# Attention with a sink and a window, then a leaky-ReLU MLP: preparing a chunk one stage earlier, in six transposes at a time, and a ramp written out by hand

## The chip, the core and the metric

The kernel runs on one NeuronCore of one Trainium2 chip. Times are device microseconds of one execution. A NeuronCore has TensorE (PE, matrix products into PSUM; PEld is its loading of weights), VectorE (DVE), ScalarE (ACT), GpSimd (POOL) and SyncE (SP, which here only issues DMAs). Each engine works through its own instructions in program order and waits for others by semaphores. PSUM has eight banks of 128 partitions x 2 KB, SBUF is the working memory.

## The reference

```python
scores = 1/sqrt(64) * q @ k.T              # q, k, v: (4, 8, 768, 64)
causal = rel >= 0                           # rel = query position - key position
stream_keep = causal & (key < 4 | rel < 64) # 4 sink keys, a window of 64
mask = causal where is_retrieval[head] else stream_keep   # is_retrieval = [1,0,1,0,0,0,1,0]
a = softmax(where(mask, scores, -1e9))
x = (a @ v), heads side by side             # (3072, 512)
h = x @ w_in                                # 512 -> 2048
out = max(0.01 * h, h) @ w_out              # 2048 -> 512
```

The list of flags says which heads are retrieval heads: 0, 2 and 6 see all earlier keys, the other five ("stream" heads) see four sink keys and a window of 64.

## The kernel before

**Chunks.** The 3072 rows are cut into eight chunks of 384 tokens, two per sequence; chunk n belongs to sequence n // 2 and is its first half (even n) or second half (odd n). Each chunk goes through four kinds of work:

- *Load and cast.* SP loads k, q and v of a chunk as float32 into four rotating buffers `f` (L66 to L82). POOL casts them to bfloat16 (`cast_chunk`, L199 to L210); v goes straight into `va`. A copy of v moved by 64 tokens, `vb`, is made by two DMAs on ACT's queue (`v_shift`, L192).
- *Preparation* (`prep_slots`, L212). For each of four pairs of heads, PE transposes k (three products with the identity, L221) into the bank `pt`; DVE copies one head's half to `kt` (L237), ACT the other (L235); then PE transposes q, and DVE copies it to `qt` (L229). `pt` is one bank with two halves; chunks 0 and 1 also use the bank `py` (`pt_tile`).
- *Attention* (`attention_slots`). A unit is one tile of scores: products into `psS` (L312 for retrieval, L347 for stream heads), the exponential on ACT (L317, L352), a mask on DVE (L321, L356), and two units later the product with v into the bank `po` (L261). An even chunk has 12 units, an odd one 21, one of which is the sink unit: DVE picks the sink keys (`ksink`, L280), PE scores them (L284). When a pair is complete, DVE divides by the sums (L373, L375), and two slots later PE transposes the result and ACT copies it to `xt` (`x_t`, L381, L382).
- *MLP.* `in_slots`: 16 steps of four products (L435) with leaky ReLU on ACT into `g` (L437). `out_slots`: 16 steps of two to four products (L449) that fill three 128-row tiles in the bank `py`; DVE copies each tile (L460), SP stores it.

PSUM's eight banks: two each for `ph` (MLP input), `psS` and `po`, one each for `py` and `pt`.

**The order.** It is written out by hand (`manual_schedule`); nothing reorders instructions afterwards, and the framework only adds the semaphores. `merge(ms, as_)` spreads one list of steps evenly over another. The stages, with chunk 0 alone first: attention of 0; input of 0 merged with preparation and attention of 1; input of 1; output of 0 merged with preparation and attention of 2; then for n = 2 to 7 the steps of input n and output n-1 in turn, merged with preparation and attention of n+1; last, output of 7. So a chunk is prepared at the start of the stage in which its attention runs. POOL also issues the weight loads, which cast while they move: half of `w_in` after the first v cast, the other half after chunk 1's q cast, then `w_out`. In the last tile of output 7 DVE copies one half and ACT the other, and two queues store them.

Of the kernel before, what the change touches and what calls it, by code (L numbers as in the profile page):

```python
# [21 lines left out]
def kernel(  # L22
# [23 lines left out]
    NCH = B * (S // CH)  # L46

# [4 lines left out]


    WIDE = 2
    qw = q.rearrange("b h (c p g) d -> b c p h (g d)", g=3, p=128)
    kw = k.rearrange("b h (c p g) d -> b c p h (g d)", g=3, p=128)
    qr = q.rearrange("b h (c g p) d -> b c p h g d", g=3, p=128)
    kr = k.rearrange("b h (c g p) d -> b c p h g d", g=3, p=128)
    vr = v.rearrange("b h (c g p) d -> b c p h g d", g=3, p=128)
# [6 lines left out]
    def load(n, nm, half=None):  # L66
        b, c = divmod(n, 2)
        if half != 1:
            stage[nm, n] = rot.tile([128, 3 * H * D], FP32, name="f", tag="f", bufs=4)
        t = stage[nm, n]  # L70
        if nm == "v" or n >= WIDE:
            tv = t.rearrange("p (g h d) -> p g h d", g=3, h=H)
            for g in range(3):
                nc.sync.dma_start(out=tv[:, g], in_={"q": qr, "k": kr, "v": vr}[nm][b, c, :, :, g])
            return
        hs = slice(0, H) if half is None else slice(4 * half, 4 * half + 4)
        src = (qw if nm == "q" else kw)[b, c]
        nc.sync.dma_start(out=t.rearrange("p (h x) -> p h x", h=H)[:, hs], in_=src[:, hs])

    def load_chunk(n):  # L80
        for nm in "kqv":
            load(n, nm)  # L82
# [18 lines left out]
    ident = one.tile([128, 128], BF16, name="ident")  # L101
    make_identity(nc, ident)
    m_win0 = one.tile([128, 6, 64], BF16, name="m_win0")

    kt = [one.tile([128, 4, 2, S], BF16, name=f"kt{i}") for i in range(2)]
    va = [one.tile([128, 6, H, D + 1], BF16, name=f"va{i}") for i in range(2)]
    vb = [one.tile([128, 5, H, D + 1], BF16, name=f"vb{i}") for i in range(2)]
    vs = [one.tile([128, H, D + 1], BF16, name=f"vs{i}") for i in range(2)]
    ksink = [one.tile([128, 4, 128], BF16, name=f"ksink{i}") for i in range(2)]
    ats = [one.tile([128, 3, 4, 64], BF16, name=f"ats{i}") for i in range(4)]  # L110
    w_in_bf = one.tile([128, KG, DF], BF16, name="w_in_bf")
    w_out_bf = one.tile([128, NG, DM], BF16, name="w_out_bf")

    def late_constants():
        nc.vector.tensor_copy(m_win0[:, 2:], m_win[:, 2:])
        nc.vector.tensor_copy(m_win0[:, 0, :], m_caus[:, 0:64])
        nc.vector.tensor_copy(m_win0[:, 1, :], m_win[:, 1, :])
        nc.vector.memset(m_win0[0:NS, 1, :], 1.0)
        nc.vector.tensor_copy(
            e_sink[:, 0 : 4 * H].rearrange("p (h r) -> p h r", r=NS),  # L120
            ident[:, 0:NS].rearrange("p (o r) -> p o r", o=1).to_broadcast([128, H, NS]),
        )

    def zeros(i):
        eng = nc.vector if i == 0 else nc.gpsimd
        eng.memset(kt[i][64:128, :, 0, :], 0.0)
        eng.memset(kt[i][0:64, :, 1, :], 0.0)
        nc.gpsimd.memset(ksink[i][:], 0.0)
        nc.gpsimd.memset(va[i][:, :, :, D], 1.0)
        nc.gpsimd.memset(vs[i][:, 0, :], 0.0)  # L130

    zeros(0)
    m_caus = one.tile([128, 128], BF16, name="m_caus")
    nc.gpsimd.memset(m_caus[:], 1.0)
    nc.gpsimd.affine_select(
        out=m_caus[:], in_=m_caus[:], compare_op=ALU.is_ge, fill=0.0,
        base=0, channel_multiplier=-1, pattern=[[1, 128]],
    )
    m_win = one.tile([128, 6, 64], BF16, name="m_win")
    nc.gpsimd.memset(m_win[:], 1.0)  # L140
    nc.gpsimd.affine_select(
        out=m_win[:], in_=m_win[:], compare_op=ALU.is_gt, fill=0.0,
        base=0, channel_multiplier=1, pattern=[[0, 6], [-1, 64]],
    )
    nc.gpsimd.affine_select(
        out=m_win[:], in_=m_win[:], compare_op=ALU.is_ge, fill=0.0,
        base=64, channel_multiplier=-1, pattern=[[0, 6], [1, 64]],
    )
    for a in ats:
        nc.gpsimd.memset(a[:, :, 1:3, :], 0.0)  # L150

    e_sink = one.tile([128, 128], BF16, name="e_sink")
    nc.gpsimd.memset(e_sink[:], 0.0)
    m_sink = one.tile([128, H, D + 1], BF16, name="m_sink")
    nc.gpsimd.memset(m_sink[:], 1.0)
    nc.gpsimd.affine_select(
        out=m_sink[:], in_=m_sink[:], compare_op=ALU.is_ge, fill=0.0,
        base=0, channel_multiplier=1, pattern=[[-NS, H], [0, D + 1]],
    )
    nc.gpsimd.affine_select(  # L160
        out=m_sink[:], in_=m_sink[:], compare_op=ALU.is_ge, fill=0.0,
        base=NS - 1, channel_multiplier=-1, pattern=[[NS, H], [0, D + 1]],
    )
    for h in range(H):
        if IS_RETR[h]:
            nc.gpsimd.memset(m_sink[:, h, :], 0.0)

    pt_n = [0]  # L170
    pt_bank = ps.tile([128, 2, 4, 128], BF16, name="pt", tag="pt", bufs=1)

    def pt_tile(n):

        pt_n[0] += 1
        if n <= 1 and pt_n[0] % 3 == 2:
            return ps.tile([128, 8, 128], BF16, name="py", tag="py", bufs=1)
        return pt_bank[:, pt_n[0] % 2]
# [4 lines left out]
    def qk_src(nm, n):  # L183
        if n >= WIDE:
            return stage[nm, n].rearrange("p (g h d) -> p g h d", h=H, g=3)
        return stage[nm, n].rearrange("p (h g d) -> p g h d", h=H, g=3)

    def cast_tile(nm, n):
        cast[nm, n] = rot.tile([128, 3, H, D], BF16, name=f"{nm}b", tag=f"{nm}b", bufs=2)
        return cast[nm, n]  # L190

# [7 lines left out]
    def cast_chunk(n, between=None):  # L199
        b, c = divmod(n, 2)  # L200
        i = b % 2
        for nm in "kq":
            tb, src = cast_tile(nm, n), qk_src(nm, n)
            for g in range(3):
                nc.gpsimd.tensor_copy(tb[:, g], src[:, g])  # L205
        if between:
            between()
        src = stage["v", n].rearrange("p (g h d) -> p g h d", g=3, h=H)
        for g in range(3):
            nc.gpsimd.tensor_copy(va[i][:, 3 * c + g, :, 0:D], src[:, g])  # L210

    def prep_slots(n):  # L212
        b, c = divmod(n, 2)
        i = b % 2
        qts[n] = rot.tile([128, 4, CH], BF16, name="qt", tag="qt", bufs=2)

        def one_pair(nm, p):
            pt = pt_tile(n)
            tb = cast[nm, n]
            for g in range(3):  # L220
                nc.tensor.transpose(pt[:, g, :], tb[:, g, 2 * p : 2 * p + 2, :], ident[:])  # L221
            pv = pt[:, 0:3, :]
            tok = lambda ap: ap.rearrange("p (g t) -> p g t", g=3)
            if n < WIDE:

                pv = pv.rearrange("p g t -> p t g")
                tok = lambda ap: ap.rearrange("p (t g) -> p t g", g=3)
            if nm == "q":
                nc.vector.tensor_copy(tok(qts[n][:, p, :]), pv)  # L229
                return  # L230
            for hh in range(2):
                r = slice(64 * hh, 64 * hh + 64)
                dst = tok(kt[i][r, p, hh, CH * c : CH * c + CH])
                if hh == 1:
                    nc.scalar.activation(out=dst, in_=pv[r], func=ACTF.Copy)  # L235
                else:
                    nc.vector.tensor_copy(dst, pv[r])  # L237

        return [lambda nm=nm, p=p: one_pair(nm, p) for p in range(4) for nm in "kq"]
# [5 lines left out]
    def attention_slots(n):  # L245
        b, c = divmod(n, 2)
        i = b % 2
        qt = lambda: qts[n]
        xts[n] = rot.tile([128, 4, CH], BF16, name="xt", tag="xt", bufs=2)
        q0 = CH * c  # L250
        po = {}
        at_sink = {}

        def av(p, hh, qi, lhsT, rhs, first, last):
            if p not in po:
                po[p] = ps.tile([128, 3, 2, D + 1], FP32, name="po", tag="po", bufs=2)
                first = True
            else:
                first = False
            o = po[p][:, qi, :, :] if hh is None else po[p][:, qi, hh, :]  # L260
            nc.tensor.matmul(o, lhsT=lhsT, rhs=rhs, start=first, stop=last, skip_group_check=True)  # L261

        sc = [0]

        def score():
            sc[0] += 1
            tag = "ph" if n == 0 and sc[0] % 2 else "psS"
            return ps.tile([128, 512], FP32, name=tag, tag=tag, bufs=2)

        units = []  # L270

        sink_lo = 128 if c == 0 else 0

# [296 lines left out]
```

## Time and profile before

| | us |
|---|---|
| median of 3 runs (lowest to highest) | 288.99 (288.77 to 289.32) |
| the profiled execution, its own time | 289.96 |
| span of its trace | 288.3 |
| PE busy in it | 249.1 (86%) |
| ACT, DVE, POOL busy | 152.4, 105.2, 59.1 |

The span runs from the first to the last instruction of one execution; the time around it is larger. Busy time of PE includes the modelled ends of its products, so that a busy PE isn't PE at its peak. The page also gives the span in 40 slices of 7.2 us, with the TensorE clock that was granted in tenths of full speed. Stretches are named by microseconds from the span's start. In this execution the stages end at about 31 (attention of chunk 0), 58 (input 0 with chunk 1), 69.5 (input 1), 96.5 (output 0 with chunk 2), 129, 158, 191, 220 and 252 (the loop, n = 2 to 6), 274 (n = 7) and 284.5 (output 7). In a line of the waits, "X <- Y: a, b, c" says that X waited a us in total for Y, b times, at longest c us.

### The profile page before, as it was taken

To read this page: it belongs to the slowest core of one execution; us is meant where nothing else is said; L and a number is where in the kernel's file an instruction comes from. 1 tells how busy PE (TensorE), PEld (TensorE's weight loads), DVE (VectorE), ACT (ScalarE), POOL (GpSimd) and SP (SyncE) were. 2 spreads that over 40 slices of the span, in tenths; PEclk is the share of its full clock that TensorE was granted. 3 is DMA by queue.
4 is the path that set the end of the run, shared out by engine and by line. 5 is a ranking of instruction groups with operands and counts; after the bars stand their busy time and mean duration, and the time that the engine had idled before them with its cause. 6 is when DMAs were issued, how large, how long until landed. Compare 5 with 4: busy or idle time off the path is not lost.

```text
span 288.3 us, 5327 instructions
## 1 busy us (share of the span) xinstructions
PE 249.1 (86%) x2111; PEld 149.2 (52%) x2140; DVE 105.2 (36%) x298; ACT 152.4 (53%) x329; POOL 59.1 (21%) x102
## 2 busy tenths in 40 slices
PE   1275699898778899999899899999898899999994
PEld 0155366554345456665466456655565466655541
DVE  6556334500246322533553333333453234311021
ACT  3345278776135457764566467745564567643300
POOL 8518930650000043002400151004300000000000
PEclk9997579999699999999999999999999999999999
DMA  8999999991000596009910990149413001010012
GB/s 188 285 261 226 208 207 210 218 191 33 6 36 36 111 228 121 36 16 218 210 38 2 211 224 23 39 95 228 118 39 82 13 36 39 0 39 36 36 73 73
DMA packets 75720, 32.36 MB, mean 112 GB/s; under 512 B 63280, under 2 KB 71728, under 8 KB 75696
## 3 DMA queue, kind: packets, MB, share of 16 engines
q1 hardware_dynamic: 70048, 25.04, 40.9%
q0 software_dynamic: 4224, 4.19, 8.6%
q10 hardware_dynamic: 1424, 2.79, 4.5%
q8 instruction: 16, 0.26, 0.4%
q14 instruction: 8, 0.07, 0.1%
HBM read 27.26 MB, written 6.29 MB: 116 GB/s over the span
## 4 chain that ended last, share of the span: by engine, by line
PE 75%; DVE 10%; ACT 8%; issue 3%; DMA 1%; ACTq 1%; DVEq 0%
PE py L449 25%; PE ph L435 25%; PE po L261 6%; PE pt L221 6%; PE psS L312 4%; ACT kt L235 4%; DVE kt L237 3%; PE pt L381 2%; PE psS L449 2%; PE psS L347 2%; ACT ats L352 2%; DVE xs L375 2%; PE psS L284 1%; DVE o L460 1%; DMA f<-in_k_dram 1%
## 5 line engine op out<-in xcount | busy, mean ns | idle before, releaser
L435 PE MATMUL ph<-xt,w_in_bf 128*128 128x384 bf16 x512 | 104.6, 331 | 0.1
L449 PE MATMUL py<-w_out_bf,g 128*128 128x512 bf16 x324 | 91.5, 386 | 2.1 <-DVE o L460 0.4
L437 ACT ACTIVATE g<-ph 128x384 bf16<-128x384 f32 x128 | 62.9, 492 | 48.6 <-PE ph L435 46.9
L435 PEld LDWEIGHTS <-w_in_bf 128*128 128x128 bf16 x512 | 46.1, 99 | 27.4 <-issue 2.6
L449 PEld LDWEIGHTS <-g 128*128 128x128 bf16 x384 | 33.9, 99 | 25.2 <-issue 2.8
L317 ACT ACTIVATE at<-psS 128x384 bf16<-128x384 f32 x81 | 39.2, 492 | 12.4 <-PE psS L312 12.2
L205 POOL CAST kb<-f 128x512 bf16<-128x512 f32 x21 | 12.8, 617 | 109.0 <-DMA f<-in_k_dram 109.0
L321 DVE TENSOR_TENSOR at<-at,m_caus 128x128 bf16<-128x128 bf16 x72 | 15.9, 248 | 40.9 <-ACT at L317 40.8
L235 ACT ACTIVATE kt<-pt 64x384 bf16<-64x384 bf16 x30 | 14.6, 486 | 30.1 <-DVE kt L237 29.8
L460 DVE COPY o<-py 128x512 f32<-128x512 f32 x21 | 14.5, 690 | 36.0 <-PE py L449 34.9
L312 PE MATMUL psS<-qt,kt 128*128 128x384 bf16 (+2 forms) x105 | 26.8, 295 | 0.1
L261 PE MATMUL po<-va,at 128*128 128x65 bf16 x252 | 22.1, 197 | 1.0 <-DVE at L321 1.0
L237 DVE COPY kt<-pt 64x384 bf16<-64x384 bf16 x30 | 11.7, 389 | 26.8 <-PE pt L221 26.8
L356 DVE TENSOR_TENSOR ats<-ats,m_win 128x384 bf16<-128x384 bf16 x40 | 15.1, 377 | 15.2 <-ACT ats L352 14.7
L382 ACT ACTIVATE xt<-pt 128x384 bf16<-128x384 bf16 x30 | 14.7, 489 | 10.8 <-PE pt L381 10.5
L221 PE MATMUL pt<-ident,qb 128*128 128x128 bf16 x84 | 10.3, 237 | 11.6 <-ACT kt L235 10.6
L229 DVE COPY qt<-pt 128x384 bf16<-128x384 bf16 x28 | 10.8, 384 | 25.7 <-PE pt L221 25.7
L261 PEld LDWEIGHTS <-at 128*128 128x128 bf16 x252 | 16.6, 100 | 6.8 <-DVE at L321 1.6
L352 ACT ACTIVATE ats<-psS 128x384 bf16<-128x384 f32 x37 | 17.9, 491 | 2.8 <-PE psS L347 2.8
L221 PEld LDWEIGHTS <-qb 128*128 128x128 bf16 x96 | 8.9, 111 | 20.1 <-issue 16.0
L205 POOL CAST qb<-f 128x512 bf16<-128x512 f32 x21 | 13.1, 629 | 27.1 <-DMA f<-in_q_dram 20.3
L221 PEld LDWEIGHTS <-kb 128*128 128x128 bf16 x96 | 9.0, 110 | 18.2 <-DVE kb L496 8.2
(75 smaller groups left out, 231.6 us busy)
## 6 DMA issues: line engine op xcount, KB each, us to landing
f<-in_v_dram SPq DMA_DIRECT2D x24, 256.0 KB, 5.4
out_dram<-o SPq DMA_DIRECT2D x23, 256.0 KB, 2.0
f<-in_k_dram SPq DMA_DIRECT2D x18, 256.0 KB, 5.3
f<-in_q_dram SPq DMA_DIRECT2D x18, 256.0 KB, 5.2
w_in_bf<-in_moe_w_in_dram POOLq DMA_DIRECT2D x4, 512.0 KB, 9.1
w_out_bf<-in_moe_w_out_dram POOLq DMA_DIRECT2D x4, 512.0 KB, 15.6
vb<-va ACTq DMA_DIRECT2D x8, 195.0 KB, 3.5
vb<-va ACTq DMA_DIRECT2D x8, 130.0 KB, 2.9
```

Of the source, the lines that this page charges most:

```text
L205: nc.gpsimd.tensor_copy(tb[:, g], src[:, g])
L221: nc.tensor.transpose(pt[:, g, :], tb[:, g, 2 * p : 2 * p + 2, :], ident[:])
L235: nc.scalar.activation(out=dst, in_=pv[r], func=ACTF.Copy)
L237: nc.vector.tensor_copy(dst, pv[r])
L261: nc.tensor.matmul(o, lhsT=lhsT, rhs=rhs, start=first, stop=last, skip_group_check=True)
L312: nc.tensor.matmul(s[:, off : off + w], lhsT=kt[i][:, p, hh, 128 * kj : 128 * kj + 128], rhs=qt()[:, p, lo:CH], start=(j == 0), stop=(j == ...
L317: nc.scalar.activation(out=a[:, 0:off], in_=s[:, 0:off], func=ACTF.Exp, scale=SM)
L352: nc.scalar.activation(out=av_, in_=s[:, 0:CH].rearrange("p (j e f) -> p j e f", j=3, e=2), func=ACTF.Exp, scale=SM)
L435: nc.tensor.matmul(ph[:, 0:CH], lhsT=w_in_bf[:, g, 128 * t : 128 * t + 128], rhs=xts[n][:, g, :], start=(g == 0), stop=(g == KG - 1))
L437: nc.scalar.activation(out=gs[n][:, t, :], in_=ph[:, 0:CH], func=ACTF.Prelu, alpha=0.01)
L449: nc.tensor.matmul(py[n][:], lhsT=gs[n][:, ng, 128 * tt : 128 * tt + 128], rhs=w_out_bf[:, ng, :], start=(ng == 0), stop=(ng == NG - 1))
L460: nc.vector.tensor_copy(o[:], py[n][:])
```

## The change

It concerns four places.

- *Preparation.* `prep_pair` transposes k and q of a pair together, six products into one bank, and then copies three pieces out; by default all three copies are DVE's. A chunk from 4 on is prepared one stage ahead, in four steps: one before the first attention slot of the chunk before it, the others behind the x transposes of a pair (`slots(extra)`). Chunk 2 is prepared ahead of its own attention, in the merged list; chunk 3 in four steps with nothing between, after chunk 2's attention. Casts and loads move one chunk ahead too.
- *Ramp.* The order of chunk 0's attention and chunk 1's preparation is written out, with transposes in `pt`, `py` and `ph`, and copies shared between DVE and ACT by a string ("vva": two on DVE, one on ACT). The second half of chunk 0's casts comes after the first scores. Weights are loaded after chunk 1's q cast; chunk 2 is loaded from POOL's queue.
- *Order of the MLP.* Eight input steps of chunk 0 are merged with chunk 1's attention; the rest and input 1 follow, then the whole output of chunk 0 in `py` and `ph`. Nine output steps of chunk 1 are merged with chunk 2, seven go into the loop.
- *Shift and end.* Chunk 0's `vb` is made by products with two shift matrices (`v_shift_pe`), four of them per tile, copied by ACT. The last tile of output 7 is computed in two halves of 256 columns in two banks.

```diff
+    def v_shift_pe():
+        for t in range(2):
+            p = bank("po", [128, 512], FP32)
+            w = D + 1
+            for o, hs in ((0, slice(1, 8, 2)), (4 * w, slice(4, 5))):
+                n = len(range(*hs.indices(8))) * w
+                for e in range(2):
+                    nc.tensor.matmul(p[:, o : o + n], lhsT=shift[:, e, :], rhs=va[0][:, t + e, hs, :],
+                                     start=(o == 0 and e == 0), stop=(e == 1), skip_group_check=True)
+            src = p[:, 0 : 4 * w].rearrange("p (h d) -> p h d", h=4)
+            nc.scalar.activation(out=vb[0][:, t, 1:8:2, :], in_=src, func=ACTF.Copy)
+            nc.scalar.activation(out=vb[0][:, t, 4, :], in_=p[:, 4 * w : 5 * w], func=ACTF.Copy)
+
+    def prep_pair(n, p, tag="pt", eng=("v", "v", "v")):
...
+        pt = bank(tag, [128, 2, 4, 128], BF16)
+        for e, nm in enumerate("kq"):
+            for g in range(3):
+                nc.tensor.transpose(pt[:, e, g, :], cast[nm, n][:, g, 2 * p : 2 * p + 2, :], ident[:])
...
+        for hh in range(2):
+            r = slice(64 * hh, 64 * hh + 64)
+            move(eng[hh], kt[i][r, p, hh, CH * c : CH * c + CH], pt[r, 0, 0:3, :])
+        move(eng[2], qts[n][:, p, :], pt[:, 1, 0:3, :])
...
+        def slots(self, extra=()):
...
+            if extra:
+                r.append(extra.pop(0))
+            for t in range(len(units) + LAG + 2):
...
+                r.append(slot)
+                if extra and t in [last[p] + LAG + 2 for p in range(4)]:
+                    r.append(extra.pop(0))
+            return r + extra
...
         for tt in range(3):
+            if halves and tt == 2:
+                slots.append(lambda: part(2, 0, NG, "py", 0, 256))
+                slots.append(lambda: part(2, 0, NG, "psS", 256, 512))
+                continue
...
-    for f in attention_slots(0):
-        f()
-    cast_chunk(1, between=lambda: [load_w("in", i) for i in (2, 3)])
-    v_shift(1)
-    for i in range(4):
-        load_w("out", i)
-    load_chunk(2)
-    zeros(1)
-    merge(in_slots(0), prep_slots(1) + attention_slots(1))
-    for f in in_slots(1):
-        f()
-    cast_chunk(2)
-    v_shift(2)
-    load_chunk(3)
-    merge(out_slots(0), prep_slots(2) + attention_slots(2))
+    a0 = Attention(0, ("psS", "ph"))
+    cast_half(0)
+    prep_pair(0, 0, "pt", "vva")
+    prep_pair(0, 1, "py", "aav")
+    u = [a0.units[h] for h in range(H)]
+    first = u[0] + u[2]
+    run([x[0] for x in first])
+    nc.gpsimd.tensor_copy(va[0][:, 0, :, 0:D], v_src(0)[:, 0])
+    nc.vector.tensor_copy(va[0][:, 1, :, 0:D], v_src(0)[:, 1])
+    nc.gpsimd.tensor_copy(va[0][:, 2, :, 0:D], v_src(0)[:, 2])
+    late_constants()
+    run([x[0] for x in u[1] + u[3]])
+    sink_mask()
+    cast_qk(1)
+    for i in range(4):
+        load_w("in", i)
+    cast_v(1)
+    for i in range(4):
+        load_w("out", i)
+    load_chunk(2, nc.gpsimd)
+    v_shift_pe()
+    run([x[1] for x in first])
+    cast_half(1)
+    prep_pair(0, 2, "pt", "vva")
+    prep_pair(0, 3, "py", "aav")
+    a0.sink()
+    second = u[4] + u[5] + u[6] + u[7]
+    run([second[0][0]], [x[1] for x in u[1] + u[3]], [second[1][0]])
+    xs0 = a0.finish(0)
+    run([second[2][0]])
+    xs1 = a0.finish(1)
+    run([second[3][0]])
+    a0.x_t(0, xs0, "pt")
+    run([second[0][1], second[4][0], second[1][1]])
+    a0.x_t(1, xs1, "py")
+    xs2 = a0.finish(2)
+    run([x[1] for x in second[2:]])
+    xs3 = a0.finish(3)
+    prep_pair(1, 0, "pt", "vva")
+    a0.x_t(2, xs2, "py")
+    prep_pair(1, 1, "ph", "aav")
+    a0.x_t(3, xs3, "pt")
+    prep_pair(1, 2, "py", "vva")
+    prep_pair(1, 3, "ph", "aav")
+    v_shift(1)
+    a1 = Attention(1).slots()
+    in0, in1 = in_slots(0), in_slots(1)
+    run(a1[0:8], merge(in0[0:8], a1[8:]))
+    zeros(1)
+    run(in1[0:8], in0[8:12], in1[8:12], in0[12:16], in1[12:16])
+    run(out_slots(0, ("py", "ph", "py")))
+    cast_qk(2)
+    cast_v(2)
+    v_shift(2)
+    load_chunk(3)
+    out1 = out_slots(1)
+    a2 = preps(2) + Attention(2).slots()
+    run(merge(out1[0:9], a2))
+    cast_qk(3)
+    cast_v(3)
+    v_shift(3)
+    load_chunk(4)
+    run(preps(3))
+    outs = out1[9:]

     for n in range(2, NCH):
         a = []
-        if n + 1 < NCH:
-            cast_chunk(n + 1)
-            v_shift(n + 1)
-            if n + 2 < NCH:
-                load_chunk(n + 2)
-            a = prep_slots(n + 1) + attention_slots(n + 1)
-        merge(weave(in_slots(n), out_slots(n - 1)), a)
-    for f in out_slots(NCH - 1, ("psS", "psS", "py"), True):
-        f()
+        if n + 2 < NCH:
+            cast_qk(n + 2)
+            cast_v(n + 2)
+            if n + 3 < NCH:
+                load_chunk(n + 3)
+        if n + 1 < NCH:
+            a = Attention(n + 1).slots(preps(n + 2) if n + 2 < NCH else ())
+        run(merge(merge(in_slots(n), outs), a))
+        if n + 2 < NCH:
+            v_shift(n + 2)
+        outs = out_slots(n) if n + 1 < NCH else out_slots(n, ("psS", "psS", "py"), True)
+    run(outs)
```

## The prediction

> **What bounds the kernel now.** I read the page's first two parts first, then the windows cut where the stages begin, then PE's waits, then the timeline of one preparation.
>
> ```profile
> PE 249.1 (86%) x2111; PEld 149.2 (52%) x2140; DVE 105.2 (36%) x298; ACT 152.4 (53%) x329; POOL 59.1 (21%) x102
> PE   1275699898778899999899899999898899999994
> PEclk9997579999699999999999999999999999999999
> ```
>
> PE is the bound: no other engine passes 53%. The 39 us that it isn't busy lie in the first 14 slices and at the end, and in two places its clock sinks. The stages (columns: stretch, its length, then PE, PEld, DVE, ACT, POOL busy, clock, DMA share, GB/s):
>
> ```profile
> 0.00:31.10 31.10, 13.63 (x136) 9.83 (x137) 18.15 (x46) 12.89 (x24) 19.75 (x44) 0.91 1.13 237
> ...
> 69.50:80.40 10.90, 8.07 (x39) 4.03 (x39) 2.47 (x7) 2.44 (x5) 0.00 (x0) 0.69 0.11 26
> 80.40:96.50 16.10, 13.12 (x144) 7.57 (x146) 9.01 (x32) 7.23 (x16) 0.00 (x0) 1.00 0.09 34
> ...
> 273.80:284.50 10.70, 10.51 (x48) 4.57 (x47) 2.18 (x4) 0.29 (x1) 0.00 (x0) 1.00 0.20 74
> ```
>
> Chunk 0's attention takes 31.1 us for 13.6 us of products; chunk 2's stage (69.5 to 96.5) 27.0 us. A dense output phase needs 10.5 us for 48 products, 0.219 each; 57.7 to 69.5 has 18 input steps in 11.8, 0.656 each. The preparations of the later stages, cut out alone:
>
> ```profile
> 96.50:105.10 8.60, 7.17 (x51) 4.05 (x52) 3.33 (x9) 3.91 (x8) 1.52 (x3) 1.00 1.09 206
> 129.00:138.20 9.20, 8.53 (x61) 4.88 (x60) 3.34 (x10) 4.40 (x9) 2.10 (x4) 1.00 1.14 211
> 158.00:167.00 9.00, 7.29 (x53) 4.12 (x53) 3.43 (x9) 4.18 (x9) 1.68 (x3) 1.00 1.05 200
> 190.80:200.00 9.20, 8.55 (x62) 4.89 (x61) 3.35 (x10) 4.40 (x9) 2.15 (x4) 1.00 1.15 212
> 220.00:228.90 8.90, 7.19 (x53) 4.06 (x52) 3.38 (x9) 4.22 (x9) 0.00 (x0) 1.00 0.28 74
> ```
>
> Length less PE busy: 1.43 + 0.67 + 1.71 + 0.65 + 1.71 = 6.2 us idle. The attention behind them loses 0.16 us where the chunk is odd, 1.0 and 1.3 where it is even. The wait, and one occurrence:
>
> ```profile
> PE pt L221 <- ACT kt L235: 10.8, 22, 1.2
> ...
> 160.94 0.35 DVE L237 COPY kt<-pt 64x384 bf16<-64x384 bf16 x1 [0.42 <-PE pt L221]
> 161.33 0.49 ACT L235 ACTIVATE kt<-pt 64x384 bf16<-64x384 bf16 x1 [1.13 <-DVE kt L237]
> 161.86 0.33 PE L221 MATMUL pt<-ident,qb 128*128 128x128 bf16 x3 [0.31 <-ACT kt L235]
> ```
>
> Three transposes, a copy on DVE, then one on ACT, and only then the next three: all on one bank, one after the other.
>
> **What the Trainium skill says.** "PSUM — Partial Sum Buffer", section "PSUM bank collisions raise a hardware error", has two engines on one bank kept apart by semaphores; the trace agrees: ACT starts 0.04 us after DVE ends, though their halves differ. "TensorE: Matmul & The Clock Gate", Part 1, has the clock halved after a window of some 3.4 us with little work, and back after a busy one. Agreed: four input products take 1.28 us at 35.2 us and 0.65 later, and after 69.5 to 73.2 us (PE some 37% occupied) the clock is 0.69. "DMA: Bandwidth & Descriptors", "Issuing engines are not separate DMA queues": loads on another queue share the same engines and save only issue time.
>
> **The change, part by part.** Times are from the span's start, and durations are rows above or timeline entries.
>
> *Preparation between scores (chunks 4 to 7).* Six transposes, then three copies on DVE, set behind the x transposes of a pair, a whole stage before use. Between x_t and a preparation there lies an input or output step (0.65) and a score; the x copy on ACT takes 0.49, so the bank is mostly free in time. DVE takes 4 x 0.36 more per stage and ACT 4 x 0.49 less (DVE 11 to 13 us busy of 29 to 33: room). Of 6.2 us I leave 1.2 (bounds 0 and 6.2). The even chunks' attention gets 31 steps to 20 slots, now 31 to 25 with eight preparations: 0.9 less idle. Stage n=2 is worse: only 23 steps beside 26 attention slots and four preparations; 39.6 to 57.7 shows what thin cover does (some 15.3 us of work in 18.1). For 24 us of work I charge 1.3. Sum **-4.6**.
>
> *The block of chunks 2 and 3.* Output of chunk 0 now runs dense, 10.5. Chunk 2's four pairs meet one bank: six transposes 0.50, then 0.35 + 0.35 + 0.36 on DVE, a cycle of 1.55 with overlap; three cycles, the last transposes and an output step: 5.6. Its attention took 16.1 with 11 output steps; seven are left, 2.6 us less work, of which I take 1.4 off, because the waits that they covered (ksink 1.1, xs 0.7 and 0.5 there) stay: 14.7. Then chunk 3's four pairs stand alone, followed by the first of chunk 4 on the same bank: 0.5 for the last x copy and four cycles, 6.7. Together 37.5, against 27.0 now. For that 28 output products (6.1) and five pairs (1.7) are done ahead: **+2.7** net. In the lone pairs PE does 1.7 us in 6.7, so its clock must fall: one window of 3.4 us at half speed in dense work, 1.7, and 0.5 for the first block (43% occupied, partly beside waits of its own): **+2.2** (bounds 0.5 and 5).
>
> *The ramp.* Followed from 5.5 us. Both operands of a pair now share a bank, so its copies start at 7.0 instead of 6.07 and go DVE, DVE, ACT. First scores 8.7 (now 15.1). DVE then has six masks, the V cast, six constants and two window masks before the second k cast: 14.3 (now 11.1). ACT has the four copies of the shift products (1.2 to 1.3 us for two DMAs of 2.9 to 3.5 that go) before the second q cast: done 15.5 (now 13.3). Pairs 2 and 3, DVE and ACT in turn: 19.1. ksink 19.1 to 19.8 (now 19.5 to 20.2): the early scores are paid back here. The rest of chunk 0, xs of the last pair at 28.6 (now 30.0); twelve copies of chunk 1 and two x copies on two engines, end 34.4; two DMA issues on ACT, first exponential of chunk 1 at 35.2. Now that point is 39.6, but with four input steps (2.6 us) and this preparation done. Eight slots cold 4.7; 17 slots with eight input steps, 10.5 us of work at the 84% of 39.6 to 57.7: 12.5; 24 dense steps 15.7. End 68.1, now 69.5: **-1.4** (bounds -5 and +3). The eight shift products themselves, at most 260 columns each, are no row of this profile; by the cold 0.32 of a 384-column product they are under 2 us on a PE that has nothing else ready there, and at nothing they change nothing.
>
> *Queues.* w_in waits on POOL for chunk 1's q cast, about 22 us; all weights use 8.6% of 288, so 25 us of the DMA engines: w_in lands near 35, first use about 40. Chunk 2's loads follow on POOL, near 61, needed at 79; nine issues at the weights' 0.75 to 0.79 are 7 us of POOL, which has nothing else then. Chunk 3's nine loads move behind three stores on SP, and wait for output of chunk 0: 79.4.
>
> ```profile
> 97.56 3.47 SPq L74 DMA_DIRECT2D f<-in_k_dram  x3
> ...
> 108.42 0.62 POOL L205 CAST qb<-f 128x512 bf16<-128x512 f32 x1 [0.59 <-DMA f<-in_q_dram]
> ```
>
> From first issue to last q cast 11.5 us: chunk 3 is cast at 90.9 (needed 99), chunk 4, whose loads stand behind it on SP, at 102 (needed 105.6). 3.6 us of cover; without it PE waits at chunk 4's first pair.
>
> *The end.* Now DVE copies half the last tile (0.42), ACT the other half after it (0.38), same bank. Two banks with half the columns leave one copy: **-0.4**. The sixteen more weight loads, 0.10 each, run beside products (PEld 4.57 of 10.7 there).
>
> Sum: -4.6 + 2.7 + 2.2 - 1.4 - 0.4 = -1.5, span 288.3 to 286.8. The profiled execution took 289.96; the median of the runs, 288.99, is 0.7 above the span: **287.5**.
>
> **Rivals.** (A) The sum, 287.5, own range 286.0 to 289.2: 0.40. (B) The ramp and block go better: chunk 1's merged part reaches 93% as in the later stages and more of the copies overlap (ramp -3.5), the clock holds (0.5): 283.7. For it: PE has 17 us idle before 31 us. Against: copies share banks: 0.24. (C) Slower, by one mechanism: the clock. Lone transposes in the block leave PE under half occupied for 5.6 and 6.7 us; if it goes cold in both and needs two windows each time, as it did from 73.2 to 80.1, 2.2 becomes 5 and the attention of chunk 2 stays at 16.1: 291.7. It decides once the block costs 2.1 us more than taken: 0.28. (D) The change doesn't do what it says: preparations between scores still wait, since x_t and they have one bank; the 4.6 is gone: 292.1. For it: ACT waits 30.2 us for DVE's kt copy in such turns. Against: a step lies between: 0.08.
>
> **How the numbers follow.** About 0.2% is what a measurement of this kernel tells from no change: 288.4 to 289.6. Faster: B and two thirds of A, 0.50. Same 0.09. Slower: C, D and the rest of A, 0.41. The range reaches from B's better part to past D: 282 to 293; A's own stands above.
>
> **What would show it.** Right: no wait of PE on pt's copies after 110 us, idle there under 0.5 us per stage; scores before 9 us and ksink near 19; a stretch near 99 to 106 us with PE a quarter busy; chunk 1's last input step near 68. Wrong: input phases over before 64 us or after 72; the clock at 0.5 for more than two windows after 79; PE waiting for chunk 4's cast.

## The result, and the profile after

The changed kernel takes 292.21 us (291.17 to 293.23, four executions) where the kernel before takes 288.88 (288.49 to 289.32) on the same chip: a ratio of 1.0115, 95% interval 1.0067 to 1.0162. It is 3.3 us slower; the forecast was 1.5 us faster. The medians here count every execution of a kernel, while the ratios leave out those that took over 1.5% longer than the fastest of the same kernel. The profiled execution took 291.40, its span is 289.7 (before 289.96 and 288.3).

The first two parts of its page, and its stages in the columns used for those of before (stretch, length, then PE, PEld, DVE, ACT, POOL busy, clock, DMA share, GB/s):

```profile
PE 250.7 (87%) x2164; PEld 153.4 (53%) x2164; DVE 114.9 (40%) x320; ACT 142.7 (49%) x311; POOL 67.3 (23%) x113
PE   0658469899976756999989999999999999999995
PEclk9999978999999985999999999999999999999999
```

```profile
0.00:30.80 30.80, 16.57 (x169) 13.16 (x170) 20.03 (x47) 14.43 (x31) 22.08 (x47) 1.00 1.01 212
30.80:41.70 10.90, 5.18 (x50) 3.28 (x48) 3.15 (x9) 5.98 (x14) 3.13 (x4) 0.84 1.18 207
...
72.60:83.00 10.40, 10.40 (x50) 4.74 (x49) 1.38 (x2) 0.49 (x1) 0.00 (x0) 1.00 0.25 78
83.00:89.40 6.40, 3.14 (x32) 1.84 (x31) 4.27 (x12) 0.00 (x0) 1.11 (x2) 1.00 0.85 179
89.40:104.80 15.40, 11.53 (x136) 7.00 (x135) 9.71 (x31) 7.19 (x16) 6.14 (x11) 1.00 1.02 191
104.80:113.10 8.30, 3.45 (x32) 2.52 (x31) 4.27 (x12) 0.00 (x0) 2.74 (x5) 0.61 1.27 203
113.10:140.00 26.90, 26.17 (x257) 16.51 (x256) 12.11 (x36) 17.62 (x41) 6.76 (x11) 0.93 0.49 95
...
168.60:198.50 29.90, 29.90 (x289) 18.77 (x288) 12.92 (x37) 18.82 (x42) 5.63 (x9) 1.00 0.58 120
```

Late in the kernel PE hardly idles: from 168.6 to 198.5 it is busy for 29.90 us of 29.90, and from the end of input 3 to the end of input 4 it now takes 29.9 us where it took 32.0. Behind the start, slices 5, 6 and 12 to 16 are where time is lost: PE is busy no more than half the time from 30.8 to 41.7, from 83.0 to 89.4 and from 104.8 to 113.1.

Cut at the same three places of the work, with the forecast beside it. The forecast of the middle two takes 0.1 for the stage n=2 out of the loops' sum (1.3 charged, less 1.43 idle, plus 0.24 of the 1.2 left over five heads), and moves chunk 4's 24 transposes, 0.056 us each from start to start, that is 1.3, from the third row to the second:

| stretch | before | after | measured | forecast |
|---|---|---|---|---|
| start to the end of input 1 | 69.6 | 72.8 | +3.2 | -1.4 |
| to the end of input 2 (block, stage n=2) | 58.3 | 67.0 | +8.7 | +6.3 |
| to the start of output 7 alone (loop) | 145.9 | 136.2 | -9.7 | -6.0 |
| to the end | 14.5 | 13.7 | -0.8 | -0.4 |
| sum | 288.3 | 289.7 | +1.4 | -1.5 |

The lower three rows err by 2.4, -3.7 and -0.4, together -1.7. The first errs by 4.6, the most. It turns the sign, and so does the second: without the one error the sum would be -3.2, without the other -1.0. The third row errs the other way; that the sum is off by only 2.9 is luck. The largest part of the first row's error is in the waits of PE between 30 and 50 us, the timeline there (start, duration, what, idle before and its end), and the transfer that PE waits for:

```profile
PE psS L306 <- ACT at L311: 3.3, 1, 3.3
PE po L263 <- DMA vb<-va: 2.4, 1, 2.4
PE pt L376 <- DVE xs L370: 0.4, 1, 0.4
```

```profile
37.98 0.51 PE L306 MATMUL psS<-qt,kt 128*128 128x384 bf16 x1
40.91 0.19 PE L263 MATMUL po<-vb,ats 128*128 128x65 bf16 x1 [2.42 <-DMA vb<-va]
...
41.67 1.35 PE L421 MATMUL ph<-xt,w_in_bf 128*128 128x384 bf16 x4
```

```profile
L198 ACTq DMA_DIRECT2D vb<-va x1: 508/508/508, 32.8 to 32.8; - x1
L199 ACTq DMA_DIRECT2D vb<-va x1: 549/549/549, 33.4 to 33.4; - x1
...
DMA to landing us min/median/max: 6.9/7.2/7.4
```

ACT issues chunk 1's two shift transfers at 32.8 and 33.4, behind its copies. They land 7 us later, at 39.7 and 40.8. The two issues themselves cost ACT nothing: its copies and then its exponentials follow one another from 32.6 on. Attention 1, whose first exponential is now at 34.0 instead of 40.4, reaches its first product with `vb` at 38.5, and PE stands. Then four input products take 1.35 us where 0.81 is the usual: from 41.8 to 45.3 the granted clock is 0.51. In the chain of work that ended last this transfer holds 3% of the span; in that of before it isn't among the lines shown.

### The profile page after: what moved, and what is told of

Read it like the earlier page. It is cut to its first block, busy times and chain, and to the rows that moved or that the text cites. A ratio compares the mean times of both kernels' runs of the same rounds, so it can differ in the third digit from the quotient of the medians.

```text
span 289.7 us, 5396 instructions
## 1 busy us (share of the span) xinstructions
PE 250.7 (87%) x2164; PEld 153.4 (53%) x2164; DVE 114.9 (40%) x320; ACT 142.7 (49%) x311; POOL 67.3 (23%) x113
## 4 chain that ended last, share of the span: by engine, by line
PE 77%; DVE 11%; ACT 5%; DMA 4%; issue 2%; ACTq 0%
PE ph L421 29%; PE py L434 23%; PE po L263 6%; PE pt L223 4%; PE psS L306 4%; DVE kt L233 3%; PE psS L434 3%; DMA vb<-va 3%; PE pt L376 2%; DVE xs L370 2%; PE psS L341 2%; ACT ats L346 1%; DVE qt L233 1%; PE psS L286 1%; DMA f<-in_k_dram 1%
## 5 line engine op out<-in xcount | busy, mean ns | idle before, releaser
L434 PE MATMUL py<-w_out_bf,g 128*128 128x512 bf16 (+1 forms) x336 | 87.2, 375 | 0.3
L311 ACT ACTIVATE at<-psS 128x384 bf16<-128x384 f32 x81 | 38.7, 490 | 31.4 <-PE psS L306 30.5
L434 PEld LDWEIGHTS <-g 128*128 128x128 bf16 x400 | 36.3, 98 | 28.7 <-issue 2.5
L439 DVE COPY o<-py 128x512 f32<-128x512 f32 (+1 forms) x21 | 14.2, 677 | 56.6 <-PE py L434 56.6
L233 DVE COPY kt<-pt 64x384 bf16<-64x384 bf16 x54 | 20.3, 377 | 19.1 <-PE pt L223 18.5
L223 PE MATMUL pt<-ident,kb 128*128 128x128 bf16 x81 | 10.0, 239 | 15.0 <-DVE qt L233 8.1
L370 DVE TENSOR_TENSOR xs<-po,linv 128x384 bf16<-128x384 f32 x32 | 17.8, 557 | 1.1
L263 PEld LDWEIGHTS <-ats 128*128 128x128 bf16 x240 | 12.4, 102 | 6.5 <-issue 2.8
L376 PE MATMUL pt<-ident,xs 128*128 128x128 bf16 x90 | 10.4, 226 | 6.1 <-DVE xs L370 5.0
L341 PEld LDWEIGHTS <-kt 128*128 128x128 bf16 x240 | 12.8, 103 | 5.3 <-issue 0.5
```

The lines of the kernel that those rows point to most:

```text
L223: nc.tensor.transpose(pt[:, e, g, :], cast[nm, n][:, g, 2 * p : 2 * p + 2, :], ident[:])
L233: nc.vector.tensor_copy(dst, src)
L263: nc.tensor.matmul(o, lhsT=lhsT, rhs=rhs, start=first, stop=False, skip_group_check=True)
L311: nc.scalar.activation(out=a[:, 0:off], in_=s[:, 0:off], func=ACTF.Exp, scale=SM)
L341: nc.tensor.matmul(s[:, 64 * m : 64 * m + 64], lhsT=kt[i][:, p, hh, k0 : k0 + 128], rhs=qts[n][:, p, 64 * m : 64 * m + 64], start=(m == 0) ...
L370: nc.vector.tensor_tensor(xs[:], po[:, :, :, 0:D], linv.to_broadcast([128, 3, 2, D]), op=ALU.mult)
```

## The experiments

Each kernel was timed beside the kernel before, whose medians in the three groups of runs were 288.5, 289.2 and 288.95 us.

### The base again

The changed kernel, unaltered.

> The changed kernel as it is, beside the three edits of it below. It gives them their base, and says how large the loss against the kernel before is over more executions: by the first measurement 1.1 percent, 3.3 us; theory (the ramp's wait for V is there in every execution, the 1.2 us of the first K cast in some of both kernels): a loss of 1 to 4 us. Rival (the first comparison caught the changed kernel at its worst): within 0.6 us of the kernel before.

292.43 us, ratio 1.0134 (1.0090 to 1.0177). The loss stands. In the profiled execution input 1 ends at 72.8, as in the first, and the wait for `vb` is 2.3; but the stretch from there to the end of input 2 takes 70.0 at a mean clock of 0.88, where the first had 67.0 at 0.92. The same code varies by 3 us there with the clock: this time it was also halved from 86.5 to 93.4, behind chunk 2's pairs, where the first execution kept 1.00. The end of input 1 didn't vary.

### Chunk 1's shift issued earlier

```diff
     cast_v(1)
+    v_shift(1, nc.sync)
...
     prep_pair(1, 3, "ph", "aav")
-    v_shift(1)
```

> The changed kernel with one edit: the two shift DMAs of chunk 1's V are issued on SP right behind the cast of V, not on ACT behind the last K copies. Theory (the products of attention 1 stand 2.4 us for the shifted V at 40.9 us, and the clock sinks behind that wait): the wait goes, input phase 1 ends near 69.5 instead of 72.6, total 287.5 to 290, that is 2.4 to 4.5 below the changed kernel. Rival (the DMA engines are full of weights until 45 us, so an earlier issue lands no earlier, or another wait takes its place): within 1 us of the changed kernel's 292.2 (291.2 at its best).

287.95 us, ratio 0.9968 (0.9939 to 0.9998). (`v_shift` takes the issuing engine as an argument here.) The same view of `vb`, up to 48 us:

```profile
L199 SPq DMA_DIRECT2D vb<-va x1: 535/535/535, 24.2 to 24.2; - x1
L200 SPq DMA_DIRECT2D vb<-va x1: 590/590/590, 24.8 to 24.8; - x1
...
DMA to landing us min/median/max: 7.3/7.5/7.6
```

The transfer is no quicker, the DMA engines being as full here from 23 to 28 us (mean share 1.21) as they were from 33.0 to 40.8 (1.17), but it lands at 31.5 and 32.4, and nothing waits for it. The clock behind it is full; 40.5 to 50 us in this kernel, then in the changed one:

```profile
40.50:50.00 9.50, 8.85 (x117) 5.99 (x115) 4.01 (x14) 8.12 (x20) 5.52 (x5) 1.00 1.14 229
```

```profile
40.50:50.00 9.50, 8.73 (x102) 6.01 (x103) 3.44 (x12) 6.47 (x16) 4.80 (x5) 0.82 1.14 231
```

Input 1 ends at 69.1 instead of 72.8: 3.7 us for a wait of 2.4. The rest fits the clock. It is halved for some 7 us in both kernels, but here in one stretch from 32.2 to 39.1, of which PE stands idle up to 34.6, waiting for an exponential, and works for 4.5; in the changed kernel from 34.9 to 38.4 and from 41.8 to 45.3, and PE works in all of the 7.0. The 2.5 us more at half speed cost some 1.25, and 2.4 and 1.25 make 3.7. ACT's queue, free of the two issues, isn't what gains: its first exponential comes at 34.1 here and at 34.0 in the changed kernel. One moved issue puts the change on the side of zero that was forecast, though barely: the interval ends at 0.9998. The rival, that an earlier issue lands no earlier or another wait takes over, falls.

### Chunk 3's preparation over two banks

```diff
-    run(preps(3))
+    for p in range(4):
+        prep_pair(3, p, ("pt", "ph")[p % 2], ("vvv", "aaa")[p % 2])
```

> The changed kernel with one edit: chunk 3's four preparations, which stand alone between attention 2 and the input phase of chunk 2, alternate over two banks and two copying engines instead of one bank and DVE. Theory (one bank and its copies set the pace, 1.75 us a pair, and the low load turns the clock down in the work behind): the stretch 104.8 to 113.1 shrinks from 8.3 to 4.5 to 5.5 us and the stage behind it loses less to the clock: 3 to 5 us below the changed kernel, 287 to 289. Rival (the clock sinks anyway, or another wait takes its place): the block alone, 2 us or less.

287.17 us, ratio 0.9939 (0.9910 to 0.9968). The four lone pairs and chunk 4's first, in the changed kernel and then in this one:

```profile
104.79 0.33 PE L223 MATMUL pt<-ident,kb 128*128 128x128 bf16 x3
104.96 0.33 PE L223 MATMUL pt<-ident,qb 128*128 128x128 bf16 x3
106.48 0.38 PE L223 MATMUL pt<-ident,kb 128*128 128x128 bf16 x3 [1.19 <-DVE qt L233]
...
108.37 0.50 PE L223 MATMUL pt<-ident,kb 128*128 128x128 bf16 x3 [1.19 <-DVE qt L233]
```

```profile
105.73 0.33 PE L223 MATMUL pt<-ident,kb 128*128 128x128 bf16 x3
...
106.06 0.33 PE L223 MATMUL ph<-ident,kb 128*128 128x128 bf16 x3
...
107.42 0.34 PE L223 MATMUL pt<-ident,kb 128*128 128x128 bf16 x3 [0.86 <-DVE qt L233]
```

Two pairs now go in the cycle of one (1.69 us in both), and the block takes 4.4 us instead of 8.3, a little less than the theory had it. Bank and copying engine were changed together; which of the two does how much wasn't run. PE's wait for `vb` in the ramp is still there (2.7), and input 1 still ends at 73.0: the gain comes behind it. From the end of input 1 to the end of input 2 it takes 63.6 us instead of 67.0.

### Both edits

> Both edits of the two runs before in one kernel. Theory: they act in different stages, so the gains add: 5.5 to 9 us below the changed kernel, 282.5 to 286, which is faster than the kernel before. Rival (one slack under both): no more than the larger of the two.

281.97 us, ratio 0.9802 (0.9743 to 0.9860), slightly below the stretch given by the theory. Off the ratio of the base come 3.3%; the edits alone bring 1.7 and 2.0. They nearly add, so they are two losses and not one slack. In the profile input 1 ends at 68.3, within 0.2 of the forecast's 68.1 (with the early shift alone it was 69.1, so that so close a match is in part luck), and from there to the end of input 2 the clock is 1.00 and the length 61.7.

### The same preparations, standing together

```diff
-            if extra:
-                r.append(extra.pop(0))
+            r += extra
+            extra = []
             for t in range(len(units) + LAG + 2):
...
-                if extra and t in [last[p] + LAG + 2 for p in range(4)]:
-                    r.append(extra.pop(0))
```

> The changed kernel with one edit: in the loop the four preparations stand together at the head of the attention list instead of one behind each pair's x transposes; still six transposes a step and one chunk ahead. Theory (a preparation gains because another pair's work lies between two uses of the bank): 4 to 8 us slower than the changed kernel, with waits of PE on the K and Q copies back at each stage's head. Rival (it is the six per step or the earlier place that gains): within 1 us of the changed kernel.

296.31 us, ratio 1.0302 (1.0236 to 1.0367), against the base's 1.0134: 1.7% or 4.9 us slower, at the lower end of the theory. In the profiles, 4.1 of it lie between the ends of input 2 and input 7 (140.5 us against 136.4), in n=3 to 5, which have a preparation; n=6 and 7, which have none, agree within 0.1. PE's waits from 115 us to the last input step, changed kernel and then this one:

```profile
PE psS L286 <- DVE ksink L276: 1.2, 3, 0.4
PE pt L376 <- DVE xs L370: 0.5, 1, 0.5
PE pt L223 <- ACT xt L377: 0.3, 1, 0.3
```

```profile
PE pt L223 <- DVE qt L233: 3.0, 6, 0.5
PE psS L286 <- DVE ksink L276: 1.2, 4, 0.5
PE pt L376 <- DVE xs L370: 1.0, 2, 0.5
PE psS L341 <- ACT at L311: 0.2, 1, 0.2
```

Six transposes at a time and a stage ahead don't remove the wait on the bank; a pair's other work between two uses does.

### The loop's part alone, on the kernel before

The kernel before, with `prep_pair` in the loop one chunk ahead behind each pair's x transposes; chunk 3 is still prepared in the old form at the head of n=2. Casts and loads move one chunk ahead with it.

```diff
-            a = prep_slots(n + 1) + attention_slots(n + 1)
+            a = (prep_slots(3) if n == 2 else []) + attention_slots(n + 1, preps(n + 2) if n + 2 < NCH else ())
```

> The kernel before with one part of the change: preparation in the loop one chunk ahead, in steps of six transposes behind each pair's x transposes (chunk 3 is still prepared at the head of the stage n=2, in the old form). Ramp, chunk 0's output beside chunk 2's preparation and the end stay as before. Theory (the loop part is worth 5 to 9 us, the ramp and the block cost 3 and 6): 280 to 284. Rival (my forecast of the loop part, 4.6 less 1.3 for the thin stage): 284 to 286. Rival (the loop gains only because its work was put into the block and the ramp): within 1 us of the kernel before.

286.66 us, ratio 0.9865 (0.9794 to 0.9936): by the medians 2.5 us, by the ratio 3.9. From the end of input 1 to the end the span has 213.7 us against 218.6 before: -4.9. That is near the -4.6 of my prediction, and the rival by which the loop gains only what was put elsewhere falls. The theory of this experiment, 280 to 284, had taken the -9.7 of the table for the loop's worth, and was too high. Between the ends of input 2 and input 7 the loop's part alone brings 7.6 us (138.1 against 145.6; the changed kernel has 136.4), and the stretch from the end of input 1 to the end of input 2, in which chunk 4 is now prepared as well, gives 2.6 of them back. Why the changed kernel has 1.7 less there wasn't traced.

### And chunk 3 between the pairs of attention 2

```diff
-    merge(out_slots(0), prep_slots(2) + attention_slots(2))
+    merge(out_slots(0), prep_slots(2) + attention_slots(2, preps(3)))
```

> The run before, with chunk 3's preparations also set between the pairs of attention 2 (beside chunk 0's output) instead of at the head of n=2. Theory (setting between works wherever attention runs beside other steps): another 1 to 2 us, 278.5 to 283. Rival (attention 2 has only few output steps to lie beside, so PE waits there as much as it did at n=2): the same as the run before within 0.7 us.

284.98 us, ratio 0.9809 (0.9732 to 0.9886), 1.7 us below the run before by medians whose executions overlap; 0.8 in the spans behind input 1. The expected total was missed, because the run it starts from had already missed its own. The medians lie with the theory and the spans near the rival's 0.7, so that the step isn't decided. The stretch from the end of input 1 to the end of input 2 takes 60.4 us here. The changed kernel does the same work there in 67.0, at a mean clock of 0.92 where this one has 0.97: that is about the price of chunk 0's output going ahead dense and chunk 3's pairs standing alone, of which the two banks took back 3.4.

### The end alone, and on top of that

```diff
+            if split and tt == 2:
+                slots += [lambda: half("py", 0), lambda: half("psS", 256)]
+                continue
```

> The kernel before with only the last output tile changed: two halves of 256 columns on two banks, each copied by DVE and stored from SP. Theory: 0.4 to 0.7 us below the kernel before (288.2 to 288.6). Rival: the same within 0.2 us.

> The run before, with the last output tile in two halves on two banks. Theory: 0.4 to 0.7 us below the run before. Rival (sixteen more matmuls cost what the copies save): the same within 0.2 us.

On the kernel before: 288.81 us, ratio 1.0026 (0.9981 to 1.0072), which by itself tells nothing. In the trace, the last stretch from the first product of output 7's dense run is 13.9 us against 14.5. On the run before: 284.23 us (281.84 to 285.67), 0.75 lower, with executions that overlap; in the span from input 7's end on, 14.2 against 14.7. A gain of 0.5 is what the traces show and the times can't.

### The first cast of K

In the ramp the first K cast took 2.31 us instead of 1.17. The timeline, before, then after:

```profile
4.15 1.77 POOL L150 MEMSET ats<- 128x384 bf16 x4
4.30 1.17 DVE L496 CAST kb<-f 128x768 bf16<-128x768 f32 x1
```

```profile
4.29 2.31 DVE L476 CAST kb<-f 128x768 bf16<-128x768 f32 x1
...
4.56 1.50 POOL L146 MEMSET ats<- 128x384 bf16 x4
```

Where the cast is short the four memsets are long, and the other way round. The kernels with the end or the loop changed, whose ramp is that of before, had the long cast (2.38 to 2.53) and ended input 1 at 70.4 to 71.5 where the profile of before has 69.6; the run with the preparations together, whose ramp is the changed kernel's, had the short one (1.20). So it goes by execution, not by the change; and with the short cast the run with the preparations together still ended input 1 at 72.6.

```diff
+    def zero_ats():
         for a in ats:
             nc.gpsimd.memset(a[:, :, 1:3, :], 0.0)
...
     nc.gpsimd.tensor_copy(va[0][:, 0, :, 0:D], v_src(0)[:, 0])
+    zero_ats()
```

> The changed kernel with one edit: POOL zeroes the four window tiles (1.5 us) behind the first cast of V, not while DVE casts the first K half. Theory (the cast takes 1.17 to 1.20 us where it gets ahead of these memsets and 2.17 to 2.53 where it falls behind them, by chance): the cast takes 1.2 us, first transposes at 5.6, input phase 1 ends 0.8 to 1.3 us earlier than in an execution of the changed kernel that has the long cast. Rival (the long cast has another reason, or a wait further on takes up the gain): cast above 2 us, or the end of input phase 1 within 0.3 us.

The same timeline, and PE's wait in the ramp:

```profile
4.50 0.69 DVE L477 CAST kb<-f 128x768 bf16<-128x768 f32 x1 [0.27 <-DMA f<-in_k_dram]
...
7.53 1.49 POOL L147 MEMSET ats<- 128x384 bf16 x4
```

```profile
PE po L264 <- DMA vb<-va: 3.2, 1, 3.2
```

The cast takes 0.69 and the first transposes come at 5.25 instead of 6.66. The time doesn't move: 291.69 us, ratio 1.0115 (1.0079 to 1.0150), input 1 ends at 73.2. Three quarters of the 1.4 are gone at once: the next transposes need q's cast, which waits for its load, and first scores come at 8.96 instead of 9.30. The remainder goes into the wait for `vb`, now 3.2 instead of 2.4, which also has the transfer landing later, at 41.4 (40.8 in the changed kernel). The rival was right for the time: where a landing decides, whatever arrives earlier waits longer.

### Chunk 0's shift by transfers

```diff
-    v_shift_pe()
+    v_shift(0)
```

> The changed kernel with chunk 0's V shifted by two DMAs from ACT as before, in place of the products and copies. Theory (I put the products at nothing and their four copies at 1.3 us of ACT): within 1 us of the changed kernel, first vb product later than 15 us or not. Rival (the shift is needed at 14 to 15 us and the DMA engines are busy with chunk 1's loads, so the products save a wait): 1 to 3 us slower.

291.08 us (288.40 to 294.13), ratio 1.0044 (1.0018 to 1.0070), against 292.43 of the base. The products save nothing here: the second half's transposes start at 15.20 in both, and the transfers, issued at 13.0 and 13.6, land at 18.4 and 19.7 without anyone waiting. The rival's loss of 1 to 3 us isn't there. Whether the transfers are a little better isn't settled: the executions of the two kernels overlap (base 290.21 to 294.13), and the profiled one shows no place for it, since input 1 ends at 73.2.

### All edits, and chunk 2 over two banks

```diff
-    a2 = preps(2) + Attention(2).slots()
+    a2 = [lambda p=p: prep_pair(2, p, ("pt", "ph")[p % 2], ("vvv", "aaa")[p % 2]) for p in range(4)]
+    a2 += Attention(2).slots()
```

This stands beside the early shift, chunk 3 over two banks and the later memsets.

> The changed kernel with the early issue of chunk 1's shift, two banks in chunk 3's preparation, the memsets moved, and chunk 2's preparation over two banks and two engines as well. Theory: 8.5 to 9.2 us from the first two, 0 to 1.2 from the memsets, and 2 to 3 of the 5.8 us that chunk 2's pairs take: 278 to 282, at least 7 us below the kernel before. Rival (attention 2 behind it only waits longer for what now comes earlier): no better than the first two edits together, 281 to 283.

282.22 us (280.02 to 282.63), ratio 0.9771 (0.9734 to 0.9807): 2.3% faster than the kernel before, and by its median no better than the two first edits, as the rival had it (by the ratio 0.3% better, with intervals that overlap). The profiled execution has a span of 278.4 against 279.9. Two of PE's waits between input 1 and input 2:

```profile
PE pt L225 <- DVE qt L235: 2.0, 3, 0.9
PE pt L225 <- POOL qb L188: 1.2, 1, 1.2
```

The wait on the bank fell from 5.1 to 2.0, and one that grows is for chunk 4's cast on POOL (0.5 with the two edits): the 3.6 us of cover that the prediction had counted for chunk 4's loads are used up here by what became faster ahead of them.

## Why the prediction was wrong

**The ramp is the step that failed.** Its chain was followed well up to chunk 1: first scores 9.30 (8.7 forecast), `ksink` 19.36 (19.1), first exponential of chunk 1 at 34.0 (35.2). But there it says "two DMA issues on ACT" and charges the issue time alone. Nobody asked when these transfers land and who waits for them. Before, they were issued at 30.6 and 31.2, landed at 37.1 and 38.3, and attention 1's first exponential came at 40.4; the change issues them 2 us later and starts that attention 6 us earlier, which leaves a wait. The two transfers of before (the last start on each line is chunk 1's) and the exponential:

```profile
L196 ACTq DMA_DIRECT2D vb<-va x2: 468/492/516, 11.3 to 30.6; - x2
L197 ACTq DMA_DIRECT2D vb<-va x2: 549/551/553, 11.9 to 31.2; - x2
...
DMA to landing us min/median/max: 5.5/6.1/7.1
```

```profile
40.39 0.87 ACT L317 ACTIVATE at<-psS 128x384 bf16<-128x384 f32 x2
```

The numbers were at hand: the landing took 5.5 to 7.1 us in the profile of before, and the weights' load that now moves into that time was worked out in the step on queues. The wait of 2.4 and the clock behind it are 3.7 of the 4.6 us, and the kernel with the early issue is faster than before, by 0.3%.

Of the remaining 0.9 some 0.3 to 0.5 may be the long first cast, by the first scores: 9.30 with it, 8.96 without the memsets beside it, 8.81 where the cast was short; the rest stays open. "Its copies start at 7.0" was 7.52, and 7.03 in the run with the short cast. Compared at an equally long cast, input 1 ends at 70.4 to 71.5 in the form of before, at 72.8 in the changed form and at 69.1 in the changed form without the wait. "SBUF — State Buffer" of the Trainium skill, section "SBUF: two separate sides", says that VectorE, in some of its operations, and GpSimd share a pair of ports which one of them holds for a whole instruction while the other stands. The traces agree with a wait of that kind, and show one cast standing through four memsets in a row: 0.69 alone, 2.31 beside 1.50 of memsets. I had taken the cast's 1.17 from one execution as fixed.

**The block was undersized.** Dense output took 10.4 (10.5). Chunk 2's pairs took 6.4 (5.6), its attention 15.4 (14.7), the lone pairs 8.3 (6.7): 40.5 against 37.5. The cycle of a pair was put at 1.55 and is 1.69 warm and 1.9 to 2.1 cold, for the clock fell inside the block and not only behind it. The mechanism is right: two banks take the lone pairs' 8.3 to 4.4. The stage behind it took 26.7 us; the sum says some 27.3 (31.4, less 7.4 for 28 output products and chunk 3's four pairs done ahead, plus 0.1, 2.2 for the clock, and 1.0 for three pairs moved in). The half clock lasted from 106.6 to 116.9, three windows of 3.4 instead of one. Rival C had the sign and nearly the time (291.7), and its mechanism in part: three windows behind the lone pairs, but in this execution none behind chunk 2's, whose attention took 15.4 and not 16.1. The row's 2.4 pass the 2.1 at which it was to decide. Still the ramp's error is the larger; the kernel with the early shift alone is faster than the kernel before, and so is the one with two banks alone.

**The loop was undersized the other way.** "Of 6.2 us I leave 1.2": in the stages n=3 to 7 PE's idle time went from 7.8 to 1.6 us (from 127.9 to 273.8 before, from 139.8 to 276.0 after, length less busy time), and two stages have none at all. Its busy time there fell by 3.4, from 138.1 to 134.6, of which 1.3 is chunk 4's preparation moved ahead; the other 2.1 may be the ends of short groups of three transposes, which the profile models, and wasn't tested. That preparations fit between the steps is shown by the run that puts them together. Rival D is out.

**The end**: -0.5 from the two halves, -0.4 forecast.

Of the signs that were to show it, these hold: no wait for the copies out of `pt` behind 113 us except 0.3 for an x copy, `ksink` near 19, chunk 4's cast in time. Others hold in part: PE idles at most 0.5 us per stage from n=4 on but 0.8 in n=3, and in the stretch of lone pairs it is busy for 3.45 of 8.3 us, more than the quarter that was named, since the clock is halved in most of it. First scores before 9 us and input 1 done near 68 didn't come. Of the signs that it was wrong two occurred: input phases over after 72, and the clock at half for "more than two windows".

## What to carry to other kernels

When a step is moved earlier, list what it reads that arrives by transfer, and price each from issue to landing at the place in the kernel where it will run, not its issue alone. A wait at a fixed landing swallows every gain ahead of it (the cast's 1.4 us gave nothing), and a gap on PE can cost more than its length: the 2.4 us here cost 3.7, with the clock halved for 3.5 us behind it. Steps that share one PSUM bank are cheap between other work and dear in a row: 4.9 us here for the same instructions in another order; if they must stand in a row, a second bank and a second copying engine took four pairs from 8.3 to 4.4.

## What the runs showed of the hardware that I had not expected

Shift transfers of 130 KB took 2.2 to 2.3 us from issue to landing at 73 us, where the DMA engines were idle, and those of 195 KB 6.9 to 7.4 at 33 us, where weights and chunk 2 were loading (7.7 to 8.2 in the run with the later memsets); issued on another queue 9 us earlier these took 7.3 to 7.6. A 128x768 cast from float32 on DVE took 0.69 us with POOL's four memsets moved away, 1.17 where it got between them, and 2.31 where it ended behind all four. And the same program, in two profiled executions, differed by 3.0 us in one stage, at a mean clock of 0.92 and 0.88 with the same instructions in the same order. The Trainium skill ("TensorE: Matmul & The Clock Gate", Part 1) has the clock set by how busy PE was in the window before. The block of lone pairs agrees (PE busy for 3.45 of 8.3 us, the clock halved from 106.6 to 116.9). Chunk 2's pairs left PE busy for 3.14 of 6.4 us in both executions, and the clock behind them fell in one and not in the other; what decides that isn't shown. So a stage that leaves PE half idle can make the time of the work behind it uncertain as well as longer.
